# Windowed attention feeding a top-1 MoE: the order of x rows, of slot 1's weights, of routing's steps and of the constants

## The chip, the cores and the metric

The kernel runs on one core of a Trainium2 chip. The metric is the device time of a launch in microseconds (us). The kernel before took 801.51 us in the median of three runs (799.58 to 802.46).

A core has these engines, each with its own instruction stream: TensorE (PE in the profile; matmuls, and transposes as matmuls), VectorE (DVE), ScalarE (ACT), GpSimd (POOL) and SyncE (SP, which here only issues transfers). Engines wait for each other by semaphores. Transfers are done by 16 DMA engines, asked for by instructions on a queue, mostly SP's.

## The reference

Two blocks, one behind the other, all in 32-bit floats:

```python
# attention: q, k, v of shape (B 8, H 8, S 576, D 64)
scores = q @ k.T / sqrt(D)
mask_plain = (rel >= 0) & (rel < 32)                       # heads 0-3
mask_dil = (rel >= 0) & (rel < 128) & (rel % 4 == 0)       # heads 4-7
attn = exp(where(mask, scores, -1e9) - max)
attn = attn / (attn.sum(-1) + 1e-9)
x = (attn @ v), heads side by side                         # 4608 x 512
# mixture of 8 experts, the best one for each row
logits = x @ w_gate                                        # 512 x 8
expert_idx = argmax(logits, axis=1)
gate_w = softmax(logits)[row, expert_idx]
y = relu(x_sorted[lo:hi] @ w1[e]) @ w2[e]                  # 512->1024->512
out = gate_w[:, None] * y, in the rows' own order
```

A row's expert is known only when the attention of all eight heads is done for that row. An expert's w1 and w2 are 2 MB each.

## The kernel before, in words

**Attention** goes by 32 units, `units` in `attention()`: a batch b (8), a head kind ty (0 plain, 1 dilated), and half of its heads hl. A unit passes through `turn` (L301; PE transposes q and k, L319 and L327), `front` (L348; the blocks of scores near the diagonal, L356 and L368), `exponentials` (ACT, L405), `norm` (the sums and reciprocals on DVE, L417 and L419; the multiply e by rec on POOL, L420), `weights` (PE transposes e, L430; DVE copies, L432), `summed` (PE multiplies by v, L445, result xo), `row_part` (PE turns the result into rows, L543) and `logit_part` (L557). The loop of `attention()` is a software pipeline over units: iteration i does `norm` of unit i-1, `front` of unit i, `summed` of unit i-3, `logit_part` of unit i-4, `weights` of unit i-2, `turn` of unit i+1 and `row_part` of unit i-3. In the first four batches the masks are added by PE with a bf16 matmul (L356), from mask packs 0 and 1; from batch 4 on DVE adds them (L390), from mask pack 2. The packs, the constants `cst` and the gate weights `wg` are loaded on POOL's queue. `row_part` of a batch's first unit has POOL write the token numbers into `rows`, which reads `cst` (L542); L537 is another POOL read of `cst`.

q, k and v of the next batch are asked for by SP as soon as the last unit that reads the old ones has been written into the program (`load_qk` L265 and L262, `load_v` L274 to L290, one buffer each). v of the dilated kind takes 13 transfers.

**Routing** is the generator `route(b)`, one for each batch: DVE copies the logits (`lgs`, L570), PE transposes them (`lg`, L573), DVE finds the best expert (`oh`), adds six running sums (`before`, L614), PE makes ranks (L620 and L627), DVE makes row addresses (`idx`), and POOL scatters the batch's rows to a DRAM buffer `bucket` that is sorted by expert (L234). At each `yield` the generator gives way to other work. After batches 1, 2, 3, 4, 5, 6 and 7, `tables(s)` makes the lists of a stage's slots: which expert, and where in `bucket` the rows start.

**The MoE** is `moe()`: 41 slots of 128 rows at most of one expert each (37 are live here). The stages are slots 0-1 (after batch 1), 2-5, 6-10, 11-14, 15-19, 20-23 and 24-40. A slot transposes its rows x (`across`, xt, L1136), does 32 matmuls for relu(x w1) (ph, L1204) and 8 for w2 (py, L1236), scales by the gate (ACT, L1247) and scatters the rows to the output (POOL, L1253).

**The order of the transfers for slots** is the list `wanted` (from L1093). Each entry is (slot, what, layer, count): it may be asked for when `done[layer]`, how many halves of ph (0) or of py (1) have been written into the program, counted over slots, has reached count, and when the slot's table is there (`where`). `fetch()` takes entries from the front of the list only, each time that a half is done or a table is ready. x goes by `fetch_x` (SP's queue up to slot 25, four buffers; 257 KB), weights by `fetch_w` (SP's queue, four transfers of 1 MB for a slot, double-buffered by the slot's parity). Since SP works in order, `wanted` also sets the place of slot transfers among the loads of q, k and v.

**The order of the whole** is made by a loop at the end that draws from three generators: `attention()`, `run_routing()` and `run_slots()`. Costs written by hand (the numbers yielded) and a rate for slots decide how many pieces of a slot lie between two pieces of attention; at most one piece of routing follows each piece of attention.

Of the kernel before, what the change touches and what calls it, by code (L numbers as in the profile page):

```python
# [23 lines left out]
N, DM, E, F = B * S, H * DH, 8, 1024  # L24
# [42 lines left out]
STAGES = [(b, READY[a] if a >= 0 else 0, READY[b]) for a, b in zip((-1, *TURNS), TURNS)]  # L67
# [8 lines left out]
J0 = STAGES[-1][1]  # L76
# [85 lines left out]
def kernel(  # L162
# [10 lines left out]
    nc = tc.nc  # L173
    packed, at, exact, mask_at, packed_last, last_at = _constants()
# [27 lines left out]
    def load_masks(i):  # L202
        nc.gpsimd.dma_start(masks[i], nc.inline_tensor(exact[i], name=f"c_mask{i}").ap())
# [41 lines left out]
    def bank(name, *dims):  # L245
        return psum.tile([128, *(dims or (512,))], F32, tag="bank", name=name)
# [168 lines left out]
    def norm(e, den):  # L415

        nc.vector.tensor_scalar(den, den, 1e-9, None, op0=OP.add)  # L417
        rec = pool.tile([128, 9], F32, tag="rec", name="rec", bufs=3)
        nc.vector.reciprocal(rec, den)  # L419
        nc.gpsimd.tensor_tensor(  # L420
            out=e, in0=e, in1=rec.unsqueeze(2).broadcast_to([128, 9, 96]), op=OP.mult
        )

# [47 lines left out]
    def attention():  # L471


        units = [(b, ty, hl) for b in range(B) for ty in range(2) for hl in range(2)]
        load_masks(0)
        for ty in range(2):
            load_qk(0, ty)
        load_masks(1)
        nc.gpsimd.dma_start(cst, nc.inline_tensor(packed, name="c_pack").ap())
        load_masks(2)  # L480
        nc.gpsimd.dma_start(wg[:, :, 0:E], moe_w_gate.rearrange("(c p) e -> p c e", p=128))
        for ty in range(2):
            load_v(0, ty)

        wrote_bucket(nc.sync.dma_start(bucket[E * CAP : NROWS], blank), 0)
        qT = {n: turn(0, 0, 0, n) for n in "qk"}
        evs, dens, eTs, xTs = {}, {}, {}, {}
        for i in range(len(units) + LAG + 3):


            ended = None
            if 0 < i <= len(units):
                norm(evs[i - 1], dens.pop(i - 1))
            if i < len(units):
                evs[i], lo, places = front(qT["q"], qT["k"], units[i][1], units[i][0] < EARLY)
            u = i - LAG - 1
            if 0 <= u < len(units):
                b2, ty2, hl2 = units[u]
                xTs[u] = pool.tile([128, S], F32, tag="xT", name="xT", bufs=3)
                for part in range(2):  # L500
                    summed(eTs[u], b2, xTs[u], ty2, hl2, part)
                del eTs[u]
                if hl2 == 1 and b2 + 1 < B:
                    load_v(b2 + 1, ty2)
            if 0 <= u - 1 < len(units):
                b2, ty2, hl2 = units[u - 1]
                logit_part(b2, 2 * ty2 + hl2, xTs.pop(u - 1))
                ended = b2 if (ty2, hl2) == (1, 1) else None
            yield 3.0, ended

            if 0 <= i - LAG < len(units):
                eTs[i - LAG] = weights(evs.pop(i - LAG))
                yield 1.1, None
            if i + 1 < len(units):
                b2, ty2, hl2 = units[i + 1]
                qT = {}
                for n in "qk":
                    qT[n] = turn(b2, ty2, hl2, n)
                    yield 0.5, None
                if hl2 == 1 and b2 + 1 < B:  # L520
                    load_qk(b2 + 1, ty2)
            if 0 <= u < len(units):
                b2, ty2, hl2 = units[u]
                row_part(b2, 2 * ty2 + hl2, xTs[u])
                yield 0.65, None

            if i < len(units):
                dens[i] = exponentials(evs[i], lo, places)
# [36 lines left out]
    def route(b):  # L565


        row = rows.pop(b)
        lgs = pool.tile([96, 2 * TT], F32, tag="lgs", name="lgs", bufs=1)
        nc.vector.tensor_copy(lgs, logits.pop(b))  # L570
        ps = bank("lg")
        for i in range(2):
            nc.tensor.transpose(  # L573
                ps[0:TT, 96 * i : 96 * i + 96], lgs[:, TT * i : TT * i + TT], ident[0:96, 0:96]
            )

        lg = ps[0:TT, 0:192].rearrange("p (i j e) -> p j i e", i=2, j=3)[:, :, :, 0:E]
        yield
        shape = [TT, NT, E]

        def small(name, *dims, dt=F32):
            return pool.tile([TT, *dims], dt, tag=name, name=name)

        def wide(a):
            return a.unsqueeze(2).broadcast_to(shape)

        def all_tiles(a):
            return a.unsqueeze(1).broadcast_to(shape)

        rev = all_tiles(const("rev", TT))  # L590
        top, best, gate = small("top", NT), small("best", NT), small("gate", NT)
        oh, dl = small("oh", NT, E), small("dl", NT, E)
        nc.vector.tensor_reduce(
            out=top.rearrange("p (j i) -> p j i", i=2), in_=lg, axis=AX, op=OP.max
        )
        nc.vector.tensor_tensor(
            out=dl.rearrange("p (j i) e -> p j i e", i=2),
            in0=lg,
            in1=top.rearrange("p (j i) -> p j i", i=2).unsqueeze(3).broadcast_to([TT, 3, 2, E]),
            op=OP.subtract,  # L600
        )

        nc.vector.scalar_tensor_tensor(
            out=oh, in0=dl, scalar=0.0, in1=rev, op0=OP.is_ge, op1=OP.mult
        )
        nc.vector.tensor_reduce(out=best, in_=oh, axis=AX, op=OP.max)
        nc.vector.tensor_tensor(out=oh, in0=rev, in1=wide(best), op=OP.is_equal)
        nc.scalar.activation(dl, dl, AF.Exp)

        for i in range(NT):
            n = b * NT + i
            nc.vector.tensor_tensor(  # L614
                out=before[:, n + 1], in0=before[:, n], in1=oh[:, i], op=OP.add
            )
        yield
        ps = bank("rank")
        rk = ps[0:TT, 0 : NT * E]
        nc.tensor.matmul(  # L620
            rk,
            lhsT=const("tri", TT),
            rhs=oh.rearrange("p t e -> p (t e)"),
            start=True,
            stop=False,
        )
        nc.tensor.matmul(  # L627
            rk,
            lhsT=const("ones", TT)[:, 0:TT],
            rhs=before[:, b * NT : b * NT + NT].rearrange("p t e -> p (t e)"),  # L630
            start=False,
            stop=True,
        )
        nc.vector.tensor_reduce(out=gate, in_=dl, axis=AX, op=OP.add)
        nc.vector.tensor_scalar(gate, gate, 1e-9, None, op0=OP.add)
        nc.vector.reciprocal(row[:, :, DM], gate)
        pick, dest, idx = small("pick", NT, E), small("dest", NT), small("idx", NT, dt=I32)
        nc.vector.tensor_tensor(
            out=pick,
            in0=rk.rearrange("p (t e) -> p t e", e=E),  # L640
            in1=all_tiles(const("ecap", TT)),
            op=OP.add,
        )
        nc.vector.tensor_tensor(out=pick, in0=pick, in1=oh, op=OP.mult)
        nc.vector.tensor_reduce(out=dest, in_=pick, axis=AX, op=OP.add)
        nc.vector.tensor_copy(idx, dest)  # L646
        for i in range(NT):
            to_bucket(idx[:, i : i + 1], row[:, i], b)
        for s, (b2, _, _) in enumerate(STAGES):
            if b2 == b:  # L650
                yield
                yield from tables(s)
# [438 lines left out]


    wanted = []  # L1093
    firsts = [j0 for _, j0, _ in STAGES]
    for j in range(NSLOT):
        x = (j, "x", 0, 2 * j - 2)

        last = j - 2 + (j - 1 in mixed)
        w = [(j, f"w{n}{h}", n - 1, 2 * last + h + 1) for n in (1, 2) for h in range(2)]
        if j - 1 in mixed:  # L1100

            wanted.insert(len(wanted) - 2, x)
        elif j < J0 and j not in firsts:

            wanted.insert(len(wanted) - 4, (j, "x", 1, 2 * j - 6))
        else:
            wanted.append(x)
        wanted += w
        if j in mixed:
            wanted += [(j, f"w{n}{h}b", n - 1, 2 * j - 1 + h) for n in (1, 2) for h in range(2)]  # L1110
    done = [0, 0]

    def fetch():
        while wanted and wanted[0][0] in where and done[wanted[0][2]] >= wanted[0][3]:
            j, what, _, _ = wanted.pop(0)
            if what == "x":
                fetch_x(j)
                continue
# [240 lines left out]
```

## Time and profile before

| | us |
|---|---|
| median of three runs | 801.51 (799.58 to 802.46) |
| the profiled execution | 802.63 |
| its span in the profile | 800.9 |
| PE busy in it | 748.6 |
| mean granted clock of PE | 0.975 |

The page's table of the span in 40 slices (20 us each) gives PE's busy tenths and granted clock, and the DMA engines' share and rate:

```profile
PE   4898898799997799999999999999999999999993
...
PEclk9999999899999799999999999999999999999997
DMA  9878689889999996799416937999992492993996
GB/s 200 178 157 196 156 233 370 190 242 281 281 305 279 359 265 193 253 311 313 147 58 199 279 122 228 309 355 383 328 319 82 150 330 97 320 307 122 332 309 219
```

The first two slices are the start, when nothing but attention can run; slots begin at 120 us (slice 6); slices 12 and 13 are the ones around 260 us.

### The profile page before, as it was taken

The page shows a single profiled execution, that of the slowest core. Times are in us where ns is not written, and L with a number is a line of the kernel's source. Part 1 is how long each engine was busy: PE and PEld are TensorE (multiplying, and loading weights), DVE is VectorE, ACT ScalarE, POOL GpSimd, SP SyncE. Part 2 cuts the span into 40 slices and gives each one's busy share as a digit, 9 for nine tenths or more (in the row PEclk, how much of TensorE's full clock was granted, in tenths as well). Part 3 has the DMA queues.
Part 4 walks back from the last instruction along what each step waited for, and adds up shares of the span by engine and source line. Part 5 has one row for each costly group of instructions (what it writes and reads, how often), then busy time and mean ns, then how long its engine had stood idle before and what let it go on. Part 6 is the DMA issues. An engine that isn't in the chain of part 4 may idle for free.

```text
span 800.9 us, 18005 instructions
## 1 busy us (share of the span) xinstructions
PE 748.6 (93%) x6838; PEld 559.4 (70%) x6838; DVE 284.6 (36%) x954; ACT 225.5 (28%) x853; POOL 146.4 (18%) x142
## 2 busy tenths in 40 slices
PE   4898898799997799999999999999999999999993
PEld 3787687488775577777777777768677374677681
DVE  1677878267334432354334411361101101101010
ACT  1896694253332132333333111000000011010000
POOL 1324433123211211113111300150000000000000
PEclk9999999899999799999999999999999999999997
DMA  9878689889999996799416937999992492993996
GB/s 200 178 157 196 156 233 370 190 242 281 281 305 279 359 265 193 253 311 313 147 58 199 279 122 228 309 355 383 328 319 82 150 330 97 320 307 122 332 309 219
DMA packets 164955, 195.39 MB, mean 244 GB/s; under 512 B 72720, under 2 KB 86688, under 8 KB 164866
## 3 DMA queue, kind: packets, MB, share of 16 engines
q1 hardware_dynamic: 153156, 169.00, 69.7%
q0 software_dynamic: 6928, 20.53, 7.2%
q10 hardware_dynamic: 4782, 4.67, 2.1%
q8 instruction: 57, 0.93, 0.5%
q14 instruction: 32, 0.26, 0.1%
HBM read 216.14 MB, written 21.54 MB: 297 GB/s over the span
## 4 chain that ended last, share of the span: by engine, by line
PE 79%; DMA 8%; ACT 5%; DVE 3%; issue 2%; another core or an unknown queue 1%; SPq 1%; POOL 0%; POOLq 0%; DVEq 0%; ACTq 0%
PE ph L1204 30%; PE py L1236 29%; PE xo L445 3%; ACT e L405 3%; PE scores L368 3%; PE weights L430 2%; DMA k<-in_k_dram 2%; DMA v<-in_v_dram 2%; PE xt L1136 2%; PE xrow L543 2%; DMA x<-bucket 2%; PE ph L1166 2%; PE py L1166 2%; PE turned L319 1%; DMA w<-in_moe_w_dram 1%
## 5 line engine op out<-in xcount | busy, mean ns | idle before, releaser
L1204 PEld LDWEIGHTS ph<-xt,w 128*128 128x128 f32 x2240 | 262.4, 193 | 19.5 <-issue 18.4
L1204 PE MATMUL ph<-xt,w 128*128 128x128 f32 x2240 | 271.7, 277 | 0.1
L1236 PE MATMUL py<-w,h 128*128 128x512 f32 x560 | 255.0, 598 | 0.0
L1236 PEld LDWEIGHTS py<-w,h 128*128 128x128 f32 x560 | 101.0, 191 | 101.4 <-issue 100.2
L1253 POOL DMA_INDIRECT out_dram<-y,to x35 | 34.6, 988 | 355.0 <-ACT y L1247 327.3
L1138 DVE COPY xt<-xt 128x512 f32<-128x512 f32 x38 | 26.1, 688 | 184.5 <-PE xt L1136 184.4
L1247 ACT ACTIVATE y<-py,x 128x512 f32<-128x512 f32 x35 | 24.0, 687 | 239.9 <-PE py L1236 177.6
L420 POOL TENSOR_TENSOR e<-e,rec 128x864 f32<-128x864 f32 x32 | 52.2, 1632 | 156.0 <-DVE rec L419 81.2
L432 DVE COPY eT<-weights 96x384 f32<-96x384 f32 x96 | 47.5, 545 | 39.8 <-PE weights L430 35.4
L405 ACT ACTIVATE e<-e,lo 128x96 f32<-128x96 f32 x144 | 51.8, 362 | 16.4 <-DVE lo L397 14.8
L234 POOL DMA_INDIRECT bucket<-rows,idx x48 | 44.5, 927 | 61.2 <-DVE idx L646 45.6
L405 ACT ACTIVATE e<-scores,lo 128x96 f32<-128x96 f32 (+1 forms) x160 | 52.5, 344 | 5.2 <-DVE lo L384 4.5
L445 PE MATMUL xo<-eT,v 96*64 96x64 f32 (+1 forms) x1216 | 45.2, 229 | 4.1 <-DMA v<-in_v_dram 4.1
L1224 DVE TENSOR_SCALAR h<-ph 128x512 f32<-128x512 f32 x35 | 24.1, 689 | 67.9 <-PE ph L1204 67.5
L445 PEld LDWEIGHTS xo<-eT,v 96*64 96x64 f32 x1216 | 40.5, 143 | 10.4 <-issue 6.6
L1215 ACT ACTIVATE h<-ph 128x512 f32<-128x512 f32 x35 | 20.8, 595 | 89.4 <-PE ph L1204 85.5
L312 ACT COPY kT<-turned 128x288 f32<-128x288 f32 x64 | 23.0, 414 | 80.2 <-PE turned L319 62.6
L430 PE MATMUL weights<-ident,e 128*96 128x128 f32 x288 | 39.2, 283 | 0.3 <-POOL e L420 0.3
L368 PE MATMUL scores<-kT,qT 64*64 64x96 f32 x1152 | 38.9, 267 | 0.1
L368 PEld LDWEIGHTS scores<-kT,qT 64*64 64x64 f32 x1152 | 33.5, 146 | 6.6 <-issue 5.0
L310 DVE TENSOR_SCALAR qT<-turned 128x288 f32<-128x288 f32 x64 | 26.5, 449 | 31.1 <-PE turned L319 16.5
L430 PEld LDWEIGHTS weights<-ident,e 128*96 128x96 f32 x288 | 32.6, 131 | 6.8 <-issue 5.7
(213 smaller groups left out, 594.2 us busy)
## 6 DMA issues: line engine op xcount, KB each, us to landing
w<-in_moe_w_dram SPq DMA_DIRECT2D x164, 1024.0 KB
x<-bucket SPq DMA_DIRECT2D x26, 257.0 KB
v<-in_v_dram SPq DMA_DIRECT2D x32, 192.0 KB
q<-in_q_dram SPq DMA_DIRECT2D x32, 144.0 KB
q<-in_q_dram SPq DMA_DIRECT2D x8, 576.0 KB
v<-in_v_dram SPq DMA_DIRECT2D x48, 96.0 KB
k<-in_k_dram SPq DMA_DIRECT2D x28, 144.0 KB
k<-in_k_dram SPq DMA_DIRECT2D x7, 576.0 KB
```

The lines of the kernel that those rows point to most:

```text
L234: nc.gpsimd.indirect_dma_start(out=bucket, out_offset=bass.IndirectOffsetOnAxis(ap=idx, axis=0), in_=rows, in_offset=None, bounds_check=NR ...
L310: nc.vector.tensor_scalar(out, in_, -SCALE, None, op0=OP.mult)
L368: nc.tensor.matmul(sc[r][64 * c : 64 * c + 64, 96 * (i % 5) : 96 * (i % 5) + 96], lhsT=qT[rows, 64 * j : 64 * j + 64], rhs=kT[rows, first_ ...
L405: nc.scalar.activation(out=e[p0:p1, i], in_=s[:, 96 * (i - i0) : 96 * (i - i0) + 96], func=AF.Exp, bias=lo[p0:p1, i : i + 1], scale=-1.0, ...
L420: nc.gpsimd.tensor_tensor(out=e, in0=e, in1=rec.unsqueeze(2).broadcast_to([128, 9, 96]), op=OP.mult)
L430: nc.tensor.transpose(tp[0:96, 128 * i : 128 * i + 128], e[:, a + i], ident)
L432: nc.vector.tensor_copy(eT, tp[0:96, 0:384])
L445: nc.tensor.matmul(xo[DH * h : DH * h + DH, at0 : at0 + nq], lhsT=vt[:, 2 * hl + r, j, :] if ty == 0 else vt[:, hl, j, DH * r : DH * r + D ...
L1166: nc.tensor.matmul(out[mine], lhsT=lhsT[:, mine], rhs=ws[:, (j + (g >= KIND[mixed[j]])) % 2, c, cols], start=c == 0, stop=c == n - 1,)
L1204: nc.tensor.matmul(ph[:, fi], lhsT=w1[:, c, 128 * f : 128 * f + 128], rhs=xt[:, c], start=c == 0, stop=c == 3,)
L1236: nc.tensor.matmul(py, lhsT=h[:, f], rhs=w2[:, f], start=f == 0, stop=f == 7)
L1253: i = nc.gpsimd.indirect_dma_start(out=out, out_offset=bass.IndirectOffsetOnAxis(ap=to, axis=0), in_=y, in_offset=None, bounds_check=N - 1 ...
```

## The change

Four edits:

- POOL's loads of `wg`, `cst` and mask pack 2 are no longer issued at the start but after the first unit's `norm` multiply.
- `route()` yields once more after the copy of the logits, and once more after the running sums.
- In `wanted`, x of every slot from 1 to 25 stands ahead of the four weights of the slot before it, if its four buffers allow (`done[1]` at least 2j-6). Before, this held for slots below 24 that aren't the first of a stage. `fetch()` now skips entries for x whose table isn't there yet, instead of stopping at them.
- Slot 1's weights may be asked for when slot 0's first half of ph has been written into the program; before, all four were asked for at once, behind slot 0's.

```diff
--- before.py
+++ after.py
@@ -417,7 +417,7 @@
         nc.vector.tensor_scalar(den, den, 1e-9, None, op0=OP.add)
         rec = pool.tile([128, 9], F32, tag="rec", name="rec", bufs=3)
         nc.vector.reciprocal(rec, den)
-        nc.gpsimd.tensor_tensor(
+        return nc.gpsimd.tensor_tensor(
             out=e, in0=e, in1=rec.unsqueeze(2).broadcast_to([128, 9, 96]), op=OP.mult
         )
 
@@ -476,9 +476,6 @@
         for ty in range(2):
             load_qk(0, ty)
         load_masks(1)
-        nc.gpsimd.dma_start(cst, nc.inline_tensor(packed, name="c_pack").ap())
-        load_masks(2)
-        nc.gpsimd.dma_start(wg[:, :, 0:E], moe_w_gate.rearrange("(c p) e -> p c e", p=128))
         for ty in range(2):
             load_v(0, ty)
 
@@ -490,7 +487,15 @@
 
             ended = None
             if 0 < i <= len(units):
-                norm(evs[i - 1], dens.pop(i - 1))
+                product = norm(evs[i - 1], dens.pop(i - 1))
+                if i == 1:
+
+                    with tc.issue_after(product.ins):
+                        nc.gpsimd.dma_start(
+                            wg[:, :, 0:E], moe_w_gate.rearrange("(c p) e -> p c e", p=128)
+                        )
+                        nc.gpsimd.dma_start(cst, nc.inline_tensor(packed, name="c_pack").ap())
+                        load_masks(2)
             if i < len(units):
                 evs[i], lo, places = front(qT["q"], qT["k"], units[i][1], units[i][0] < EARLY)
             u = i - LAG - 1
@@ -568,6 +573,7 @@
         row = rows.pop(b)
         lgs = pool.tile([96, 2 * TT], F32, tag="lgs", name="lgs", bufs=1)
         nc.vector.tensor_copy(lgs, logits.pop(b))
+        yield
         ps = bank("lg")
         for i in range(2):
             nc.tensor.transpose(
@@ -614,6 +620,7 @@
             nc.vector.tensor_tensor(
                 out=before[:, n + 1], in0=before[:, n], in1=oh[:, i], op=OP.add
             )
+        yield
         yield
         ps = bank("rank")
         rk = ps[0:TT, 0 : NT * E]
@@ -1091,18 +1098,20 @@
 
 
     wanted = []
-    firsts = [j0 for _, j0, _ in STAGES]
     for j in range(NSLOT):
         x = (j, "x", 0, 2 * j - 2)
 
         last = j - 2 + (j - 1 in mixed)
         w = [(j, f"w{n}{h}", n - 1, 2 * last + h + 1) for n in (1, 2) for h in range(2)]
+        if j == 1:
+
+            w = [(j, what, 0, max(1, n)) for _, what, _, n in w]
         if j - 1 in mixed:
 
             wanted.insert(len(wanted) - 2, x)
-        elif j < J0 and j not in firsts:
-
-            wanted.insert(len(wanted) - 4, (j, "x", 1, 2 * j - 6))
+        elif 0 < j < J0 + 2:
+
+            wanted.insert(len(wanted) - 4, (j, "x", 1, max(0, 2 * j - 6)))
         else:
             wanted.append(x)
         wanted += w
@@ -1111,8 +1120,15 @@
     done = [0, 0]
 
     def fetch():
-        while wanted and wanted[0][0] in where and done[wanted[0][2]] >= wanted[0][3]:
-            j, what, _, _ = wanted.pop(0)
+        while wanted:
+
+            at0 = 0
+            while at0 < len(wanted) - 1 and wanted[at0][1] == "x" and wanted[at0][0] not in where:
+                at0 += 1
+            j, what, layer, n = wanted[at0]
+            if j not in where or done[layer] < n:
+                return
+            wanted.pop(at0)
             if what == "x":
                 fetch_x(j)
                 continue
```

## The prediction

> **What bounds the kernel now.** I read the page's engine rows first, then TensorE's (PE's) waits, the windows around the large ones, and SyncE's (SP's) timeline to see what those waited for. PE is the bound on average, so the only thing to gain is the time in which PE stands still or runs at half clock.
>
> ```profile
> PE 748.6 (93%) x6838; PEld 559.4 (70%) x6838; DVE 284.6 (36%) x954; ACT 225.5 (28%) x853; POOL 146.4 (18%) x142
> ```
>
> The waits of PE (what for, us in total, times, longest):
>
> ```profile
> PE xt L1136 <- DMA x<-bucket: 10.4, 1, 10.4
> PE turned L319 <- DMA k<-in_k_dram: 7.9, 3, 3.6
> PE turned L319 <- DMA q<-in_q_dram: 5.0, 2, 4.7
> PE xo L445 <- DMA v<-in_v_dram: 4.1, 1, 4.1
> ...
> PE rank L627 <- DVE before L614: 2.6, 2, 1.4
> PE rank L627 <- DMA w<-in_moe_w_dram: 2.0, 1, 2.0
> ```
>
> Two holes dominate: one wait for x, one for v. The windows place them (PE, PEld, DVE, ACT, POOL busy, PE clock, DMA share, GB/s):
>
> ```profile
> 130.00:140.00 10.00, 10.00 (x147) 9.32 (x146) 7.66 (x23) 5.67 (x24) 2.75 (x3) 1.00 1.06 351
> 140.00:150.00 10.00, 5.86 (x31) 4.01 (x32) 3.41 (x8) 3.33 (x18) 3.50 (x3) 0.69 0.71 191
> ...
> 260.00:270.00 10.00, 4.13 (x22) 4.13 (x23) 1.42 (x3) 0.00 (x0) 0.00 (x0) 0.50 1.06 321
> 270.00:280.00 10.00, 10.00 (x120) 7.62 (x120) 7.63 (x39) 1.97 (x5) 5.53 (x6) 1.00 1.05 392
> ```
>
> Each hole is followed by work at half clock, so it costs more than its idle time. After 270 us PE is full to the last slots; every microsecond won before that moves the end. SP's timeline (start, duration of a run of issues) says what delayed the two transfers:
>
> ```profile
> 112.06 1.55 SPq L1070 DMA_DIRECT2D x<-bucket  x2
> 114.41 14.07 SPq L1089 DMA_DIRECT2D w<-in_moe_w_dram  x8
> 128.58 19.51 SPq L290 DMA_DIRECT2D v<-in_v_dram  x13
> ...
> 166.35 1.57 SPq L1070 DMA_DIRECT2D x<-bucket  x2
> ...
> 233.17 12.21 SPq L290 DMA_DIRECT2D v<-in_v_dram  x13
> 245.78 1.93 SPq L1089 DMA_DIRECT2D w<-in_moe_w_dram  x3
> ...
> 251.00 1.84 SPq L1070 DMA_DIRECT2D x<-bucket  x2
> ```
>
> The v of 128.58 stands behind eight weight transfers (two slots, 8 MB); x6 and x7, of 251.00, behind slot 5's weights and behind v, q and k of a later batch, though the table that x6 reads is ready at 189. x6 lands at 263 to 266 us, after 14.8 us in a queue full of packets.
>
> **What the Trainium skill says.** "DMA: Bandwidth & Descriptors", Queues, rings and completion order: descriptors of one queue are consumed in the order of its ring. The trace agrees: x6 takes 14.8 us although 257 KB at 321 GB/s is under 1 us. So an earlier place in SP's order is an earlier landing, at the cost of what is passed. "TensorE: Matmul & The Clock Gate", What's actually happening: an idle window halves the clock and a busy one restores it; the trace has 0.50 and 0.69 in the two windows above. "SBUF — State Buffer", Who interferes with whom: VectorE and GpSimd share a port pair, held for a whole instruction, and a two-input VectorE operation contends. The trace agrees, in VectorE's and then POOL's timeline (start, duration, and idle before):
>
> ```profile
> 62.77 1.96 DVE L614 TENSOR_TENSOR before<-before,oh 96x8 f32<-96x8 f32 x3
> ```
>
> ```profile
> 62.88 1.63 POOL L420 TENSOR_TENSOR e<-e,rec 128x864 f32<-128x864 f32 x1 [4.09 <-DVE rows L636]
> ```
>
> Those three sums have a median of 163 ns and one lasts 1567 ns beside the multiply. "Trainium Kernel Development and Optimization", Key Constraints: transfers of SP, ACT and POOL run on the same 16 DMA engines, so moving POOL's start loads helps only by taking bytes out of the way.
>
> **The change, part by part** (the order of the changed program's instructions can be read without running it).
>
> *Rows of a stage's first slot.* Before, x6 is behind slot 5's four weights, v (13 issues), q and k; after, it follows slot 4's weights and x7 follows slot 5's. x6 is then issued some 20 us earlier (about 231 us in the old times). Its table has been ready 40 us, and the buffer is free since four x tiles rotate and x2 is consumed at 173. Even 15 us in the queue lands it ahead of 255. What is passed: slot 5's weights and v wait for 257 KB, under 1 us. Gain: the 10.4 us of the wait, plus half-clock work of 265.9 to 270 (4.1 us busy at 0.50, so 2.0 lost): **-12.4**. The same for x11, x15, x20: none has a wait in the list, so 0; x24 and x25 pass the weights too, and land some 40 us early: 0.
>
> *Slot 1's weights later.* SP's order becomes x0, x1, four weights, v (13), q and k, v of batch 4, then slot 1's four. The v hole loses its cause: 4 MB less ahead, at the 391 GB/s of 120 to 130 us, 10.7 us, against a wait of 4.1. Gain: 4.1 idle; the half clock from 145.7 to 150.5 (4.8 at half, 2.4); and about 1.7 of small gaps between attention and slot matmuls in the same stretch (elapsed less busy work, 138 to 161): -8.2. But the bytes are not fewer. x2 was issued at 166.35 behind everything, and all of it is still ahead of x2 (v, q, k, slot 1's 4 MB, v of batch 4, q and k of batch 5): I expect x2 at 163 to 169, mid 166. PE reached x2's transposes at 173.3; less 8.2 and the routing below that is about 163. So what is late next is x2: a new wait of 3 (0 to 6) with 1 of half clock, **-4.2** net (-8.2 to -1). Slot 1's weights themselves are needed at about 159 and, after 16 or so issues that used to be behind them, land at about 146 to 154: 5 to 13 us to spare. Slots 5 to 7 run with a smaller lead (1 to 4 us at 5 and 6, estimated), now that PE is 17 us earlier and DMA share was 1.05 there: **+0.5** (0 to 5).
>
> *Routing farther apart.* A yield puts other PE work between the copy of the logits and its transposes, and between the running sums and their rank matmul. For the first two batches the sums are still locked out by the multiply of 1.63 us (row above) ahead of rank, and the scores end at the same time: 0 (-1 to +0.5). At the third, rank waited 2.0 (122.95 to 124.94; the row blames w, but it is the DVE sums), lg about 0.9, with slot work now between: -1.3 (-2 to -0.5). Later batches, whose waits are under 0.3: -0.3 together. In all **-1.6**. The DVE time of routing itself doesn't change; a yield postpones tables by one attention step (some 2 us), and tables are ready 40 us early except the first.
>
> *Constants and masks later.* 397 KB (165 cst, 216 masks, 16 gate) leave the first 10 us, when k's wait ended at 15.78. At 200 GB/s (the page's first slices) that is 2 us, of which k, partly ahead of it, gets about 1.2. They come back behind the first multiply (23.99 + 1.63) as traffic at 25 to 29, where the next k was awaited until 35.87. On POOL, the rows' copy that reads cst now stands ahead of the second multiply (28.51), which PE's transposes need at about 32: cst issued at 26 with a landing of 3 reaches just in time; with the 7.8 that the page gives for it in the crowded first microseconds, the second multiply would be some 2 us late (the +1 below, half of it covered by k's wait to 35.87). Gate weights are first read at 33.2. **-0.8** (-1.7 to +1). Masks 2 serve batches 4 on, near 150 us: 0; if it were late there, PE wouldn't notice, since VectorE adds them.
>
> Sum: -12.4 - 4.2 + 0.5 - 1.6 - 0.8 = -18.5. The profiled execution was 802.63 (span 800.9), which gives 784.1; the median of the runs is 801.51, 1.1 lower, which gives **783.0**.
>
> **The rivals.**
> *All holes vanish and nothing comes in their place.* x2 in time (another -4), no wait at slots 5 to 7 (-0.5), routing at its best (-1.5), start -1.7: -25.4, 776. For it: DMA share 0.93 to 0.96 rather than 1.05 at 150 to 170, so there is slack. Against: x2's queue.
> *The queue becomes the bound.* The DMA engines, full from 110 to 140 and at 1.04 to 1.06 from 250 to 280, give back half: x2 6 late plus clock 1, weights of slots 5 to 9 late by 5 in all: -18.5 + 3 + 4.5 = -11, 790.5. For it: the rows above; against: after 290 the share falls to 0.15 to 0.6.
> *Slower: slot 1's weights late.* They are asked for when slot 0's first half is done and behind v and q, k; if these block SP (v and q wait there for free buffers), slot 1 stands still, 1 us for 1 us, and half clock follows. With 9 us to spare on the mean and 18.5 to lose, it decides from a landing near 187 instead of 150. For it: SP's issues took 19.51 us for one v. Against: the buffers it waits for are freed by attention, which runs on.
> *It doesn't do what it says.* x2 is still behind slot 1's weights, so "ahead of weights" is not true there; if the x6 wait were bound by bytes, not by place, it would stay: about -5, and 796. Against: the table ready at 189.
>
> **From cases to numbers.** Forecast 0.60 (its own range 779 to 788), all gone 0.13, the queue bound 0.17, place doesn't matter 0.04, no net change 0.02, slower 0.04. A measurement of this kernel can tell about 0.3%, 2.4 us. Faster is the sum of the first four, 0.94, less a little for their tails: 0.93. The range is 774 to 792.
>
> **What would show it right or wrong.** The wait for x at 255 to 266 is gone and no 10 us window from 250 to 280 is below 9 busy. The v wait at 141 to 146 is gone; a wait of xt for x near 163 stands in its place, 0 to 6 us. Rank's wait at 123 is under 0.7, the early ones stay near 1. First transposes of k at 14.3 to 15. The order after 280 is the old one, some 18 earlier. I am wrong if slot 1's first ph waits for w, if the second multiply comes after 32 us, or if weights of slots 5 to 9 are awaited by more than 5 us.

## The result, and the profile after

The changed kernel takes 788.86 us in the median of six executions (785.32 to 794.69), the kernel before 801.02 in the median of six (798.43 to 802.46): a ratio of 0.9861, with a 95% interval from 0.9814 to 0.9907. The medians differ by 12.2 us, where 18.5 were forecast; 788.86 lies inside the range of 774 to 792, well above its middle, and 0.9 us above what the forecast gave as its own part of it (779 to 788). The profiled execution is the fastest of the six, 785.32 us with a span of 783.5; the sum, which was made against a profiled execution, gave 784.1.

PE's row on the page of the changed kernel, and then its waits (total us, times, longest):

```profile
PE 745.9 (95%) x6838; PEld 557.7 (71%) x6838; DVE 279.4 (36%) x954; ACT 226.5 (29%) x853; POOL 146.3 (19%) x142
```

```profile
PE rank L634 <- DVE before L620: 4.2, 3, 1.5
PE xt L1152 <- DMA x<-bucket: 3.2, 1, 3.2
PE rank L627 <- DVE gate L641: 1.5, 1, 1.5
PE rank L627 <- ACT dl L614: 1.5, 1, 1.5
...
PE ph L1220 <- DMA w<-in_moe_w_dram: 0.9, 1, 0.9
```

PE's busy time has changed by under 3 us (748.6 before); the span lost 17.4, most of it idle time. The wait for v is gone, the wait for x of 10.4 us too. In their place stand a wait for x of 3.2 us and one for weights of 0.9. The windows (PE, PEld, DVE, ACT, POOL busy, PE clock, DMA share, GB/s) place them:

```profile
140.00:150.00 10.00, 9.04 (x116) 5.60 (x115) 5.45 (x14) 4.75 (x19) 3.46 (x3) 1.00 0.99 252
160.00:170.00 10.00, 6.76 (x48) 6.26 (x47) 1.08 (x4) 2.99 (x15) 1.62 (x1) 0.83 0.75 206
...
250.00:260.00 10.00, 10.00 (x132) 8.24 (x131) 6.08 (x21) 4.74 (x22) 5.53 (x6) 1.00 1.05 309
260.00:270.00 10.00, 9.07 (x52) 5.67 (x51) 4.37 (x26) 0.69 (x1) 2.82 (x3) 1.00 1.05 333
```

The new hole ends at 165.6 us: x2, as forecast. The DMA engines are as full as before around 260 (1.05), and there PE now runs without a margin. SP's timeline (start, duration of a run of issues) shows what stands ahead of whom:

```profile
146.73 10.89 SPq L262 DMA_DIRECT2D q<-in_q_dram  x4
157.74 3.77 SPq L262 DMA_DIRECT2D k<-in_k_dram  x4
162.87 1.57 SPq L1077 DMA_DIRECT2D x<-bucket  x2
...
226.18 13.47 SPq L290 DMA_DIRECT2D v<-in_v_dram  x13
...
246.23 16.15 SPq L1096 DMA_DIRECT2D w<-in_moe_w_dram  x4
```

x2 is behind eight transfers of q and k that took SP 15 us to put on the queue. The four weights of 246.23 are slot 6's; PE waits for the first of them at 266.4. They are behind 13 transfers of v, which the forecast had in the way of x6, but not of slot 6's weights.

### The profile page after: what moved, and what is told of

Read it like the earlier page. It is cut to its first block, busy times and chain, and to the rows that moved or that the text cites. A ratio compares the mean times of both kernels' runs of the same rounds, so it can differ in the third digit from the quotient of the medians.

```text
span 783.5 us, 18001 instructions
## 1 busy us (share of the span) xinstructions
PE 745.9 (95%) x6838; PEld 557.7 (71%) x6838; DVE 279.4 (36%) x954; ACT 226.5 (29%) x853; POOL 146.3 (19%) x142
## 5 line engine op out<-in xcount | busy, mean ns | idle before, releaser
L405 ACT ACTIVATE e<-e,lo 128x96 f32<-128x96 f32 x144 | 51.8, 362 | 14.2 <-DVE lo L397 12.7
L368 PE MATMUL scores<-kT,qT 64*64 64x96 f32 x1152 | 36.5, 255 | 0.1
L368 PEld LDWEIGHTS scores<-kT,qT 64*64 64x64 f32 x1152 | 31.1, 138 | 6.6 <-issue 3.8
```

What stands on the lines that cost most here:

```text
L368: nc.tensor.matmul(sc[r][64 * c : 64 * c + 64, 96 * (i % 5) : 96 * (i % 5) + 96], lhsT=qT[rows, 64 * j : 64 * j + 64], rhs=kT[rows, first_ ...
L405: nc.scalar.activation(out=e[p0:p1, i], in_=s[:, 96 * (i - i0) : 96 * (i - i0) + 96], func=AF.Exp, bias=lo[p0:p1, i : i + 1], scale=-1.0, ...
```

## The experiments

Times are medians. Each ratio, with its 95% interval, is to the kernel before, run on the same chip in the same comparison; it is taken over the executions of both and isn't the quotient of the two medians, from which it can differ by some thousandths (0.9883 beside 787.94 and 801.51, whose quotient is 0.983). Waits and windows are from one profiled execution of each kernel.

### The changed kernel again, and with three of its edits undone, on a second chip

`whole_again` is the changed kernel. The other three undo one edit each:

```diff
 # no_yield: both added lines out of route()
-        yield
 # no_w1: slot 1's weights right behind slot 0's
-        if j == 1:
-            w = [(j, what, 0, max(1, n)) for _, what, _, n in w]
 # no_const: cst, mask pack 2 and wg loaded at the start again
-                    with tc.issue_after(product.ins):
-                        nc.gpsimd.dma_start(wg ...); nc.gpsimd.dma_start(cst ...); load_masks(2)
```

> The changed kernel itself once more, for what varies in it. Its six executions went from 785.3 to 794.7, and the profiled one was the fastest of them. Theory S1 (clock): slower executions have the same waits (x2 about 3 us, w 1 us) and more PE time at half clock, where short routing waits before 170 us happen to fill an idle window; a profile of a slower one shows two to four more half-clock stretches[...], each costing 1 to 2 us. Theory S2 (queue): a slower execution has longer waits for x2 and for weights of slots 5 to 8, 5 us or more above those of the profile at hand. Ratio to before 0.982 to 0.990 under both.

> The changed kernel without the two added yields. The prediction's sum has the yields worth 1.6 us: so 1.6 us slower than the whole change (0 to 3), with the wait of rank at the third batch back at about 2.0 us and the waits of lg at 0.9 each. Rival: the yields cost time in the early batches (waits of rank for its sums are 4.2 us in the changed kernel, 1.2 to 1.5 each, and batch 1 has a stretch of half clock at 90 to 100 us), and this kernel is 1 to 3 us faster than the whole change.

> The changed kernel with slot 1's weights where they were, right behind slot 0's. The prediction's sum: the wait of xo for v comes back (4 us and half clock behind it, 8 in all), the wait of xt for x2 (3.2 us) goes, net 4 us slower than the whole change. Rival: both waits are one and the same queue time, since x2 still has the same bytes ahead of it, and this kernel is within 1 us of the whole change, with a wait for v of 4 us or more and none for x2.

> The changed kernel with POOL's loads of constants, mask pack 2 and gate weights back at the start. The prediction's sum: 0.8 us slower than the whole change. Rival 1: the start is 2.6 to 3 us behind (the first k at 15.8 again instead of 12.4), none of it is made good, and this kernel is 3 us slower. Rival 2: the 3 us are made good at the next wait that the queue sets (k of batch 1, or x2 at 165), so that it is 0 to 1 us slower although all of its first 100 us come 3 us later.

This chip differs from the first: the kernel before takes 843.28 us on it (46 executions, 840.49 to 848.46). The changed kernel took 847.04, 1.0041 [1.0026, 1.0055]; without yields 843.29, 1.0005 [0.9989, 1.0021]; without the later weights 847.5, 1.0060 [1.0039, 1.0081]; without the moved loads 848.55, 1.0061 [1.0037, 1.0085]. So here the change wins nothing, and costs 0.4%. The waits of PE in `whole_again` suggest why the first chip's reasons don't apply:

```profile
PE ph L1220 <- issue: 14.8, 17, 2.2
PE turned L319 <- ACT xT L459: 8.3, 2, 4.2
PE xo L445 <- issue: 7.7, 11, 1.1
...
PE logits L562 <- issue: 4.0, 5, 1.1
PE weights L430 <- issue: 3.5, 4, 1.1
```

"Issue" is idle time in which PE waited for no semaphore that the trace shows: 30.0 us in the four rows of that name, against none in the first chip's list. It comes in bursts, one to three instructions at a time, in the middle of a group of the same kind, as in PE's timeline here:

```profile
147.25 0.38 PE L430 MATMUL weights<-ident,e 128*96 128x128 f32 x2 [0.94 <-issue]
148.73 0.29 PE L430 MATMUL weights<-ident,e 128*96 128x128 f32 x1 [1.10 <-issue]
```

I read that as PE's own instructions arriving late; this is not shown, and what would make them late was not found. It isn't PE alone: the 8.3 us for ScalarE's copy xT stand in the list because ScalarE itself stood idle, 36.4 us in all ahead of that copy, until something that the trace doesn't name. A PE that is held up like this can be expected to come later than its transfers, and none of the four traces has a wait for x, for v or for weights. `no_w1` is telling, since its slot 1 weights stand ahead of v as they did before the change, and v is not awaited. The whole change was about such waits. There is no trace of the kernel before on this chip, so whether x6 too was in time there is open. One difference is clear: without the two yields the kernel is 3.7 us faster here than with them, and the intervals don't overlap, as the rival for `no_yield` had it. Otherwise these four runs don't separate the theories written for them, since the waits that those are about are absent.

### The kernel before, the changed one, and two edits alone, on a third chip

```diff
 # only_x: the list's condition and the new fetch() alone
-        elif j < J0 and j not in firsts:
-            wanted.insert(len(wanted) - 4, (j, "x", 1, 2 * j - 6))
+        elif 0 < j < J0 + 2:
+            wanted.insert(len(wanted) - 4, (j, "x", 1, max(0, 2 * j - 6)))
 # only_w1: this alone
+        if j == 1:
+            w = [(j, what, 0, max(1, n)) for _, what, _, n in w]
```

> The kernel before, unchanged, for its trace beside the next three. Where the chip is like that of the first comparison: 799 to 803 us, a wait for x6 of 10 us at 256 to 266, one for v of 4 us at 142. Where it is like that of the runs just made, in which PE stood idle for some 40 us in places where it waited for nothing but its own instructions: 843 us; then theory I (instructions are late on that chip for every kernel) expects such idle time here too, 20 us or more, and shorter waits for x6 and v than in the first trace, since a PE that is held up elsewhere needs them later. The rival, that the changed order alone brings these stops, expects none here.

> The changed kernel, unchanged, on the chip of the run before. Like the first chip: 0.982 to 0.990 of before, x6's wait gone, x2 awaited for about 3 us. Like the second: 1.00 to 1.006 of before, with 20 us or more of idle PE behind no wait but the issue of instructions.

> Before, with the edit of the list of transfers alone (x of a stage's first slot ahead of the weights, and the skipping of rows without a table). The prediction's sum: -12.4 us (0.9845 of before), the wait of xt for x6 gone, the wait for v at 142 as before. Rival: v, passed by nothing new, and the weights of slots 5 to 8, each behind one x more, take back 5 us or more as waits for w: -7 or less.

> Before, with slot 1's weights asked for later alone. The prediction's sum: the wait of xo for v (4 us, 8 with what follows) gone, a wait of xt for x2 of 3 us in its place, net -4.2 us (0.995). Rival A: the gain is swallowed at x6, whose landing is set by the bytes ahead of it, so that its wait grows by what was won: 0 (1.000). Rival B: the two early waits are one queue time: x2 is awaited for as long as v was, 0 already at 170 us.

This chip is like the first: before took 801.51 us, and of its four traces only that of `only_x` has idle time behind issue, 1.8 us. The kernel before against itself gave 1.0016 [0.9994, 1.0038], which shows how far a ratio can lie from 1 with nothing changed; its trace has the same two holes, the one for v of 3.4 us and the one for x6 larger (806.53 us, the profiled execution):

```profile
PE xt L1136 <- DMA x<-bucket: 14.4, 1, 14.4
```

The changed kernel took 787.94 us, 0.9883 [0.9799, 0.9966] (four executions, of 787.74 to 798.12). Its waits in this trace:

```profile
PE ph L1220 <- DMA w<-in_moe_w_dram: 3.4, 1, 3.4
PE xt L1152 <- DMA x<-bucket: 2.5, 1, 2.5
```

Up to slot 6's rows this execution is 2.3 us ahead of the first profiled one (xt of slot 6 starts at 248.6 against 250.9). Slot 6's weights are then awaited 3.4 us instead of 0.9, PE is busy 6.56 of the 10 us from 260 to 270 (the prediction had 9 or more as a sign of being right), its clock is 0.95 and 0.88 in that window and the next, and slot 7's rows come at 273.9 against 272.0. This execution is quicker before slot 6 and not behind it.

`only_x` took 792.58 us, 0.9893 [0.9856, 0.9931]. In its trace x6's wait is gone (xt of slot 6 starts at 254.6 against 265.9 before), slot 5's w2 matmuls are 12.7 us ahead, and 10.1 us of that reach the end. A wait of 0.9 us for slot 6's weights is new, and the lead is 11.1 us at 295 us in the old times; where the last 1 us goes was not found. v is awaited 6.0 us.

`only_w1` took 803.61 us, 1.0038 [1.0020, 1.0057]: no faster, rather a little slower, which its trace doesn't explain. Waits and windows of that trace:

```profile
PE xt L1139 <- DMA x<-bucket: 17.9, 2, 14.6
```

```profile
140.00:150.00 10.00, 10.00 (x132) 7.33 (x131) 6.33 (x16) 5.68 (x23) 1.63 (x1) 1.00 0.93 209
...
250.00:260.00 10.00, 1.11 (x12) 0.61 (x11) 0.00 (x0) 0.60 (x1) 0.00 (x0) 0.81 1.02 331
```

The v hole is filled (10.00 busy from 140 to 150), a wait of 3.3 us for x2 comes in its place, and the rows of slots 3 to 5 come 4.3 to 4.6 us ahead of before, close to the 4.2 of the sum. Then x6 takes all of it: it lands when it did (265.7 us, 265.9 before), and is awaited 14.6 us. From there on the trace is 0.2 us ahead. Rival A holds: alone, the edit of slot 1's weights wins nothing.

### x2 in its place, and the other two edits undone, on another chip

```diff
 # x2_early, on top of the changed kernel: q and k of batch 5 behind x2 and x3
-                if hl2 == 1 and b2 + 1 < B:
+                if hl2 == 1 and b2 + 1 < B and (b2, ty2) != (4, 0):
                     load_qk(b2 + 1, ty2)
...
 # at the end of fetch_x(j)
+        if j == 3:
+            load_qk(5, 0)
```

`no_yield_2` and `no_const_2` are the kernels shown above.

> The changed kernel with x2 and x3 moved on SP's queue ahead of the eight transfers of q and k of batch 5, which come right behind them. In the changed kernel x2 was issued at 162.9, behind those eight (146.7 to 161.5), and was awaited 2.5 to 3.2 us. Theory P (place): x2 is issued near 147, lands by 158, the wait goes, and 2 to 4 us of it reach the end: 0.982 to 0.985 of before where the whole change is 0.986 to 0.988. Theory Q (bytes): the weights of slots 5 to 8 come at the rate of DMA engines that are full from 185 to 270 (share 0.98 to 1.07), so what is won at x2 is waited for again at slot 6's weights (0.9 and 3.4 us in two traces of the changed kernel, then 3 to 6), and the end moves by less than 1 us.

> The changed kernel without the two added yields, once more, where PE isn't held up by late instructions. The prediction's sum: 1.6 us slower than the whole change (0.988 to 0.990 of before). Rival 1, from the run before (3.7 us faster than the whole change on that chip): the yields cost time, and this is 2 to 4 us faster (0.982 to 0.984). Rival 2: all that routing wins or loses before 130 us is taken up by the wait for x2 or for slot 6's weights: within 1 us.

> The changed kernel with POOL's loads back at the start, once more. The prediction's sum: 0.8 us slower than the whole change. In two traces of the changed kernel all work up to 90 us came 1.7 to 2.6 us earlier than before. Rival 1: that reaches the end: 2 to 3 us slower (0.989 to 0.991 of before). Rival 2: it is taken up by the later wait for x2 or for slot 6's weights, as the 4.4 us of slot 1's weights alone were by x6: 0 to 1 us slower, with a shorter wait for x2.

Before took 802.21 us on this fourth chip; the changed kernel itself was not run on this chip, so its ratios on the first and the third, 0.9861 and 0.9883, have to stand in. `x2_early` took 790.65, 0.9854 [0.9822, 0.9885]: not clearly better than the changed kernel. SP's timeline and the waits of its trace:

```profile
148.75 2.14 SPq L1077 DMA_DIRECT2D x<-bucket  x2
150.99 7.57 SPq L262 DMA_DIRECT2D q<-in_q_dram  x4
...
248.66 14.66 SPq L1098 DMA_DIRECT2D w<-in_moe_w_dram  x4
```

```profile
PE ph L1222 <- DMA w<-in_moe_w_dram: 4.6, 1, 4.6
```

x2 is issued 14 us earlier and no longer awaited; slot 3's rows come 4.8 us before those of the changed kernel's first trace (183.7 against 188.5). At slot 6 the weights are awaited 4.6 us, with the clock at 0.83 from 260 to 280, and slot 7's rows come 2.8 us behind it (274.8 against 272.0). PE gets to slot 6's first weights at 266.4, 264.1 and 262.6 us in the traces of the changed kernel on the first and the third chip and of `x2_early`, and goes on at 267.3, 267.6 and 267.2: in these three traces they are there at the same time, whatever PE won ahead of them. That is theory Q: the wait wasn't removed, it was moved to the next thing on the same queue.

`no_yield_2` took 789.86 us, 0.9849 [0.9815, 0.9882]: on this chip the yields make no difference that these runs can tell. Its trace, the fastest of its six executions, has no wait for slot 6's weights at all; attention and slots alternate differently in it, so it can't be laid beside the others at that place. `no_const_2` took 795.93 (one of its six executions took 2760 us, which the ratio leaves out), 0.9891 [0.9854, 0.9928]. That is 2.4 us above the changed kernel's ratio on the first chip and 0.6 above that on the third, and the intervals overlap: what the moved loads are worth isn't settled. Its trace is 10.0 us behind the changed kernel's first from slot 13 on, but sets the slowest of its other five executions against the fastest of six. In it the first k is awaited until 16.1 again, and x2 (4.2 us) and slot 6's weights (3.9 us) longer, with half clock behind each.

### A better version

`v5_later`, run on the third chip, has the order of `x2_early`, and takes away what stands ahead of slot 6's weights:

```diff
 # on top of x2_early, in attention()
-                if hl2 == 1 and b2 + 1 < B:
+                if hl2 == 1 and b2 + 1 < B and (b2, ty2) != (4, 1):
                     load_v(b2 + 1, ty2)
...
 # in fetch(), behind the fetch_w of w1's halves
+                if (j, what) == (6, "w11"):
+                    load_v(5, 1)
```

> The changed kernel with x2 and x3 ahead of q and k of batch 5 as in the run of x2, and with the 13 transfers of v of batch 5 (dilated heads), which stood between slot 5's weights, placed behind the first two of slot 6's instead. They took SP 226.2 to 239.6 us in the changed kernel and their v is first read near 276. If the queue's bytes and places set the arrival of slot 6's first weights, as the x2 run showed (x2's wait gone, slot 6's weights awaited 4.6 us), these weights now come 8 us or more earlier, that wait goes too, and the end moves: 4 to 8 us faster than the x2 run, 0.975 to 0.981 of before. Rival: the next bytes are late in their turn (v of batch 5 at 270 to 276, or slot 7's weights), with a wait of 4 us or more for one of them: 0.984 to 0.987, no better than the changed kernel. A run held up by late instructions would tell neither by its time; then the waits before 290 us decide.

It took 785.41 us (780.88 to 790.52) against 803.91 for before: 0.9779 [0.9740, 0.9817], with 18.5 us between the medians, and the profiled execution 781.61 us. That it beats the kernel before is clear, and it lies where it was expected: its interval ends just below where that of `x2_early` begins (0.9822), though that run was on another chip. It also ends just above the lower end of the changed kernel's (0.9814), so that it is better than the changed kernel is likely, not beyond doubt. The later v without the earlier x2 was not run. SP's timeline and a window of its trace:

```profile
239.18 2.66 SPq L1098 DMA_DIRECT2D w<-in_moe_w_dram  x2
241.88 23.92 SPq L290 DMA_DIRECT2D v<-in_v_dram  x13
```

```profile
260.00:270.00 10.00, 9.98 (x128) 9.36 (x127) 2.84 (x7) 2.46 (x5) 2.92 (x3) 1.00 0.63 174
```

Slot 6's first weights are issued at 239 instead of 246 or 249, PE is full from 260 to 270, and slot 7's rows come at 265.1, 7.0 us ahead of the changed kernel's first trace. v of batch 5, moved back by some 16 us, isn't awaited: the one wait for v in this trace, 0.6 us, is at 134 us, for an earlier batch. Slot 7's weights are awaited 1.8 us, until 287.9. At the end 4.0 of the 7.0 us are left.

## Why the prediction was right, and where not

- **What bounds the kernel.** Right in the main: most of what moved was idle PE before 270 us. But not "every microsecond won before that moves the end": of 12.7 us at slot 7's rows 10.1 reached it in `only_x`, and of 7.0 (against the changed kernel) 4.0 in `v5_later`.
- **x of a stage's first slot, -12.4.** Right in mechanism, and in size at its place: slot 5's w2 matmuls came 12.7 us ahead with this edit alone. Of that, 10.1 reached the end of its trace, and the medians say 8.9 (801.51 to 792.58). Part of the rest went to the term "slots 5 to 7".
- **Slot 1's weights, -4.2 net.** Right in mechanism and size: the v hole gone, x2 awaited 3.2, 2.5 and 3.3 us in three traces, where 3 (0 to 6) was written; some 4.4 us ahead at slots 3 to 5. What the sum didn't say is that it wins nothing without the first edit. The Trainium skill's "DMA: Bandwidth & Descriptors", Queues, rings and completion order, has each DMA engine take a ring's descriptors in order, so that the place on the queue counts, and `x2_early` agrees: a transfer issued 14 us earlier on the same queue was no longer waited for, with the same bytes moved.
- **Slots 5 to 7 with a smaller lead, +0.5 (0 to 5).** This is the term that failed, by its size. Slot 6's first weights were awaited 0.9 and 3.4 us in the two traces of the changed kernel on chips like the first, with half clock behind the larger one, and 3.9 and 4.6 in two variants. 0.5 was taken from the lucky end of its range. With some 4 us there instead, the sum comes to -15, nearer to the medians' -12.2 than -18.5; the remaining 3 us are open. The step behind it: I added up the gains ahead of slot 6 as if each reached the end, while the DMA share of 1.04 to 1.06 from 250 to 280 us, quoted in the prediction, says that the queue has no room there. The rival in which the queue becomes the bound (790.5) described the median better than the forecast; its place was right (slots 5 to 9), its x2 of 6 us was not.
- **Routing, -1.6.** Seen in the waits, not in the times. The wait for lgs (2.6 us) is gone, but rank waits 4.2 us for its sums where it waited 4.6 in all (2.6 and 2.0), and the other rank 1.5 and 1.5 where it waited 1.2 and 1.1: 7.2 us in all, where it was 9.5. The third batch's wait is 1.2, not under 0.7. With the yields the ratio is 0.9861 (first chip), without them 0.9849 (fourth), and on the second chip the yields cost 3.7 us. One reading there was loose: the 163 ns are the median of all 48 running sums in that trace, not of the three shown.
- **Constants and masks, -0.8 (-1.7 to +1).** Too small at the start. PE's timeline of the changed kernel has the first transposes of k at 12.39, not at 14.3 to 15, and waiting for DVE rather than for k:

```profile
12.39 1.20 PE L319 MATMUL turned<-ident,k 96*128 96x96 f32 x6 [0.71 <-DVE qT L310]
```

  Up to 90 us all work came 2.6 us earlier in this trace and 1.7 in the third chip's. The step from 15.78 to 12.39 is 3.4 us, more than the whole 2 us that I had for the bytes, of which I gave k 1.2; what the loads cost k besides their bytes isn't shown. How much of it reaches the end isn't settled either (`no_const_2`, above).
- **From a profile to the median.** The forecast took the profiled execution of before to lie 1.1 us above the median, and the same of after. But the execution that was profiled after was the fastest of six, 3.5 us below their median. So it is partly luck that the sum, 784.1, comes within 1.2 us of it: routing isn't seen in it, the constants gave more, and all six executions lie above the forecast of 783.0. The six span 9.4 us; the six of before span 4.0, but 41 of before on the third chip span 10.1. The two traces of the changed kernel differ in slot 6's wait and the half clock behind it (above), and in the routing of batch 1, from 90 to 100 us: the clock there is 0.54 in the first and 0.83 in the other, and in the first the lead over before fell from 2.6 to 0.7 us. The mean granted clock of every execution is on record: 0.974 for the slowest of the six (794.7 us) and 0.981 to 0.985 for the three fastest, 0.973 for the 798.1 us on the third chip and 0.981 to 0.982 for the other three. More time at half clock goes with a slower execution, then; whether idle PE or other causes start it isn't settled, as the slow ones have no trace.

## What to carry to other kernels

In this kernel a wait for a transfer on a full queue that works in order couldn't be priced alone. Ask what is next on the same queue, and follow the gain past it, as long as the DMA share stays near 1. An edit that gained 4 us in front of a hole that another transfer set gained nothing while that hole was open (`only_w1`), and with it closed the next transfer became what PE waited for (`x2_early`). So look for work that the queue carries long before its use (here v, issued at 226 and read at 276), and put it behind what is late.

## What the runs showed of the hardware that was not expected

- The comparisons on different chips differ by more than the change. In the one on the second chip the kernel before took 843.28 us in 46 executions, against 801 to 804 in the others, and in the changed kernel PE stood idle for 30 us without a semaphore to wait for, 18 us of them in gaps of 0.9 to 1.2 us between single instructions or pairs. The trace's instruction packets, 57 of 16 KB, took no longer there (median 1.04 us, against 1.00 in the changed kernel's first trace). Whether it is the chip or the hour isn't shown, since that chip was used once. The same change had a ratio of 0.986 on the first chip and 1.004 there.
- In the trace of `v5_later`, putting 13 transfers of v on the queue took SP 9.3 us at 164 us (batch 4) and 23.9 at 242 (batch 5, as many bytes). What differs is what SP had just put on the queue: two weight transfers of 1 MB just ahead of the first, six within 18 us ahead of the second. That a full queue holds up the engine that issues is the likely reading; no run varies it alone.
